# Loading w1 in full rows, a 512-column xn, and row tiles that trade banks, in a one-core attention and MLP kernel

## Chip, core, metric

The kernel runs on one NeuronCore of one Trainium2 chip, in one launch. The metric is the device time of one execution in microseconds (us). Before the change it is 152.92 us, the median of 3 runs (152.84 to 153.02). Each run also carries a state: "slow" when it is over 1.5% above the fastest run of the same kernel. Ratios use fast runs alone; a median that is quoted is of all runs of a kernel, and says so where one of them was slow. The profiled executions are single runs, and profile times count from the first instruction, so a profile's span is about 1.7 us shorter than the time of the same run.

## The reference

```
x:[1,2048,448] bf16,  H=16 heads of 28,  F=1792
xn    = layernorm(x)
q,k,v = xn @ wqkv
phi_q = concat(softmax(q @ w_phi), softmax(-q @ w_phi))      # per head, 56 features; phi_k likewise
kv, z = sum_s phi_k * v,  sum_s phi_k
att   = ((phi_q @ kv) / (phi_q @ z + 1e-6)) @ wo
mlp   = silu(xn @ w1) @ w2
out   = x + att + mlp
```

## The kernel before

S = 2048 is cut into 16 row tiles of 128 rows ("tiles" 0 to 15) and 4 chunks of four tiles. D = 448 is seven blocks of 64. Every matmul is issued as a pair: one on array rows 0 to 63 ("LO", q = 0) and one on rows 64 to 127 ("HI", q = 1), with the two results in two different banks of PSUM, the memory that matmuls write to. A list scheduler in the kernel source orders each engine's instructions when the program is built. After that the order is fixed. In the profile after, VectorE kept to its list: two copies whose input PE had written by 19.9 us started at 22.33, behind an instruction that waited for a load until 21.77.

The names used below: F1 is xn @ w1 with silu, F2 is h @ w2, V and QK are the projections, FT and FM prepare the weights of QK (transpose the qk half of wqkv, multiply by w_phi), X brings xn into transposed form (xT), U and WO are the attention output at the end.

xT must hold each 64-block on both halves of the partitions. So xn is written with every block twice, 896 columns, and from tile 4 on one transposing DMA on the sync engine (SP) turns a whole tile:

```python
def LN_b(t, parts=((0, NS),), od=False):                      # NS = 7 blocks
    ...
        dst = xnd[:, t % NX, a * 128:b * 128].rearrange("p (s r n) -> p s r n", s=b - a, r=2)
        src = xs.rearrange("p (s n) -> p s n", s=NS)[:, a:b, None, :].broadcast_to([128, b - a, 2, 64])
        ... e.tensor_scalar(dst, src, mean, rstd, subtract, mult)      # VectorE

def X_dma(t):                                                 # tiles 4..15
    dstx = xT[:, c % NXC, :, j * 128:(j + 1) * 128]
    src = xnd[:, t % NX, :]
    P.dma(lambda e: e.dma_start_transpose(out=dstx, in_=src), ..., issue=1230.0, fixed=3200.0)
```

w1 lies as halves: LO partitions hold columns 0 to 895 and HI partitions 896 to 1791, so each load covers 64 partitions. The bulk loads (x of tiles 4 to 7 among them) follow at marks in the stream of matmuls:

```python
w1v = B_w1.rearrange("(s p) f -> p s f", p=64)
def load_w1(a, b, after=None):
    load(w1_sb[LO, a:b, :], w1v[:, a:b, 0:896], ...)
    load(w1_sb[HI, a:b, :], w1v[:, a:b, 896:1792], ..., eng="act")
...
# F1, a pair: one 64-block s, two output tiles
pair([(bank(2 * sl + q)[:, 0:n], w1_sb[HALF[q], s, i * 128:(i + 1) * 128],
       xT[HALF[q], c % NXC, s, ...], s == 0, s == NS - 1) for q in range(2)], n, "f1")
...
load(wv_sb[LO], ..., after=marks[2])
load(wv_sb[HI], ..., after=marks[3])
load_x(4, 6, after=marks[4])
load(w2_sb[:, 0:7], ..., after=marks[5])
load_x(6, 8, after=marks[7])
load(w2_sb[:, 7:14], ..., after=marks[8])
...
for t in range(4, 8):
    LN(t); X_dma(t)                 # layernorm and transpose for chunk 1
```

The order of the tensor engine's stages at the start is: F1 of chunk 0 with FT and FM inside, V, QK and F2 of chunk 0, then F1 of chunk 1.

The softmax here doesn't subtract the row's maximum and nothing guards it: scores larger than these inputs give would overflow.

## Time and profile before

| | before |
|---|---|
| time, median | 152.92 us |
| span of the profile | 151.6 us |
| PE busy | 142.8 us |
| first F1 matmul | 6.67 us |
| first V, first QK matmul | 24.29, 27.04 us |
| first F1 matmul of chunk 1 | 37.63 us |
| from the first QK matmul to the end ("the tail") | 124.5 us |

The page's table of busy time and its chain of work that ended last (shares of the span), of the kernel before:

```profile
PE 142.8 (94%) x2118; PEld 88.3 (58%) x2118; DVE 96.7 (64%) x179; ACT 84.4 (56%) x106; POOL 83.9 (55%) x95
...
PE 91%; DMA 4%; issue 1%; ACT 1%; DVE 0%; DVEq 0%; ACTq 0%
```

The same chain in order of time, before; columns are start, us, what:

```profile
20.71 1.57 issue
22.28 125.66 PE psum L432 x1774
```

From 22.28 to 147.94 us the tensor engine (PE) works without a break. What is lost lies before that. The PE timeline, before; columns are start, busy us, engine, line, operation, output<-input, shapes, count, and in brackets the idle time before the group and what ended it:

```profile
6.67 0.62 PE L432 MATMUL psum<-xT,w_sb 64*128 64x128 bf16 x16 [0.74 <-DMA w_sb<-in_B_w_dram]
...
8.73 1.04 PE L432 MATMUL psum<-xT,w_sb 64*128 64x128 bf16 x16 [1.32 <-DMA w_sb<-in_B_w_dram]
...
22.28 0.23 PE L432 MATMUL psum<-BD,phT 64*128 64x56 bf16 x4 [1.57 <-issue]
...
24.29 1.49 PE L432 MATMUL psum<-wv_sb,xT 64*128 64x448 bf16 x14
...
27.04 2.82 PE L432 MATMUL psum<-wqk,xT 64*128 64x448 bf16 x28
...
37.63 6.22 PE L432 MATMUL psum<-xT,w_sb 64*128 64x512 bf16 x56
```

Two waits for w1 and one stall stand before 22.28 us. Between the two w1 waits and after them the granted clock (the share of the tensor engine's full clock that the profile reports as granted) falls too: 0.5 from 8.04 to 11.45 us. The windows table, before; columns are stretch, its length, then busy us (and instructions) of PE, PEld, DVE, ACT, POOL, then the granted PE clock, the DMA share and GB/s:

```profile
8.70:12.04 3.34, 3.31 (x62) 3.06 (x63) 1.94 (x8) 0.33 (x1) 0.55 (x1) 0.59 1.06 287
```

```profile
L570 SPq DMA_TRANSPOSE xT<-xnd x4: 1286/1296/1327, 29.2 to 33.3; - x4
DMA to landing us min/median/max: 3.0/3.1/3.2
```

Each of these transposing DMAs holds the SP queue for 1.30 us. Four of them for chunk 1 take 5.34 us in a row. The last one, issued at 33.26, landed at 36.22 us by the trace. F1 of chunk 1 starts at 37.63. So there is a deadline here, and it is met with 1.4 us to spare.

### The profile page before, as it was taken

How to read it: one execution, taken by the hardware profiler on the slowest of the kernel's cores; microseconds unless marked ns; L12 is line 12 of the kernel's file. 1: busy time of each engine (PE TensorE's matmuls, PEld its weight loads, DVE VectorE, ACT ScalarE, POOL GpSimd, SP SyncE). 2: the span in 40 equal slices, each digit the busy share in tenths (PEclk: the TensorE clock that was granted, in tenths of full speed). 3: DMA queues.
4: the chain of work that ended last, by engine and by line, in shares of the span. 5: the costliest groups of instructions: out<-in, count | busy, mean ns of one | idle time of the engine just before them, and what ended most of it. 6: DMA issues, size and time to landing. Idle time of an engine off the chain costs nothing.

```text
span 151.6 us, 4915 instructions
## 1 busy us (share of the span) xinstructions
PE 142.8 (94%) x2118; PEld 88.3 (58%) x2118; DVE 96.7 (64%) x179; ACT 84.4 (56%) x106; POOL 83.9 (55%) x95
## 2 busy tenths in 40 slices
PE   6769959999999999999999999999999999999990
PEld 2379957555556555555555556565556666666550
DVE  2747548699998376990129697874047694848633
ACT  3115748988955976895779587678573102011110
POOL 3307000706999996969902899999991402222130
PEclk9959999999999999999999999999999999999999
DMA  3996895093772997239781023333376344863323
GB/s 79 255 272 178 227 316 206 4 169 73 225 93 42 137 173 153 69 97 157 158 183 35 0 63 80 69 74 69 73 107 79 81 123 124 49 191 73 102 84 121
DMA packets 43678, 18.42 MB, mean 122 GB/s; under 512 B 36680, under 2 KB 43400, under 8 KB 43656
## 3 DMA queue, kind: packets, MB, share of 16 engines
q1 hardware_dynamic: 43000, 17.19, 53.6%
q10 hardware_dynamic: 656, 0.92, 2.4%
q8 instruction: 17, 0.28, 0.8%
q14 instruction: 5, 0.04, 0.1%
HBM read 7.48 MB, written 1.84 MB: 61 GB/s over the span
## 4 chain that ended last, share of the span: by engine, by line
PE 91%; DMA 4%; issue 1%; ACT 1%; DVE 0%; DVEq 0%; ACTq 0%
PE psum L432 90%; DMA w_sb<-in_B_w_dram 4%; PE psum L445 1%; ACT L496 1%; DVE x_sb L752 0%; DVEq L1020 0%; ACTq L463 0%
## 5 line engine op out<-in xcount | busy, mean ns | idle before, releaser
L640 POOL TENSOR_TENSOR E<-E,Rk 128x896 bf16<-128x896 bf16 x32 | 53.3, 1699 | 8.7 <-ACT E L450 6.3
L432 PE MATMUL psum<-xT,w_sb 64*128 64x512 bf16 (+2 forms) x522 | 48.1, 331 | 2.1 <-DMA w_sb<-in_B_w_dram 2.1
L432 PE MATMUL psum<-w_sb,hT 64*128 64x448 bf16 x448 | 45.2, 349 | 0.0
L450 ACT ACTIVATE hT<-psum 128x1024 bf16<-128x1024 f32 (+1 forms) x32 | 28.9, 917 | 12.8 <-PE psum L432 12.0
L432 PEld LDWEIGHTS psum<-xT,w_sb 64*128 64x128 bf16 x522 | 26.5, 98 | 15.4 <-DMA w_sb<-in_B_w_dram 1.7
L432 PEld LDWEIGHTS psum<-w_sb,hT 64*128 64x128 bf16 x448 | 24.1, 94 | 16.6
L633 DVE TENSOR_REDUCE Sk<-E 128x64 f32<-128x1792 bf16 x16 | 31.9, 2004 | 2.4 <-ACT E L450 2.3
L450 ACT ACTIVATE E<-psum 128x896 bf16<-128x896 f32 x32 | 27.4, 916 | 6.2 <-PE psum L432 6.0
L450 ACT ACTIVATE xT<-psum 128x448 f32<-128x448 f32 (+2 forms) x12 | 5.7, 481 | 33.8 <-PE psum L432 21.9
L432 PE MATMUL psum<-wqk,xT 64*128 64x448 bf16 x224 | 23.6, 349 | 0.0
L704 POOL TENSOR_TENSOR xT<-xT,x_sb 128x448 f32<-128x448 f32 x8 | 8.3, 1034 | 24.9 <-ACT xT L450 24.9
L432 PEld LDWEIGHTS psum<-wqk,xT 64*128 64x128 bf16 x224 | 12.2, 94 | 8.6
L557 DVE TENSOR_SCALAR xnd<-x_sb,mv,rstd 128x896 bf16<-128x896 bf16 (+2 forms) x18 | 11.1, 656 | 9.1 <-POOL rstd L547 9.1
L547 POOL TENSOR_TENSOR rstd<-ve,neghalf 128x1 f32<-128x1 f32 x16 | 8.8, 564 | 8.7 <-DVE ve L545 8.4
L692 POOL TENSOR_TENSOR Ye<-Ye,x_sb 128x448 f32<-128x448 f32 x8 | 8.2, 1035 | 7.7 <-DVE Ye L690 7.7
L432 PE MATMUL psum<-wv_sb,xT 64*128 64x448 bf16 x112 | 11.9, 349 | 0.0
L539 DVE BATCH_NORM_STATS2 st<-x_sb 128x6 f32<-128x448 bf16 x16 | 9.5, 608 | 3.4 <-DMA x_sb<-in_A_x_dram 3.4
L432 PE MATMUL psum<-wo_sb,E 64*128 64x448 bf16 x112 | 11.3, 349 | 0.0
L690 DVE TENSOR_TENSOR Ye<-psum,Ye 128x448 f32<-128x448 f32 x8 | 5.0, 621 | 9.0 <-ACT Ye L450 8.9
L729 DVE TENSOR_TENSOR E<-psum,rden 128x224 bf16<-128x224 f32 x32 | 10.3, 383 | 0.3
L545 POOL TENSOR_SCALAR ve<-mv 128x1 f32<-128x1 f32 x12 | 2.3, 216 | 12.4 <-DVE mv L543 12.4
L432 PEld LDWEIGHTS psum<-wo_sb,E 64*128 64x128 bf16 x112 | 6.2, 94 | 4.4
(42 smaller groups left out, 102.0 us busy)
## 6 DMA issues: line engine op xcount, KB each, us to landing
out_dram<-x_sb SPq DMA_DIRECT2D x8, 224.0 KB, 2.2
w_sb<-in_B_w_dram SPq DMA_DIRECT2D x2, 784.0 KB, 6.7
x_sb<-in_A_x_dram SPq DMA_DIRECT2D x2, 448.0 KB, 4.5
wv_sb<-in_A_wqkv_dram SPq DMA_DIRECT2D x2, 392.0 KB, 4.7
wo_sb<-in_A_wo_dram SPq DMA_DIRECT2D x14, 56.0 KB, 2.2
w_sb<-in_B_w_dram SPq DMA_DIRECT2D x3, 224.0 KB, 5.4
w_sb<-in_B_w_dram ACTq DMA_DIRECT2D x3, 224.0 KB, 6.1
phT<-in_A_wqkv_dram SPq DMA_DIRECT2D x1, 448.0 KB, 5.6
```

Source lines behind the costliest of these rows:

```text
L432: ins = e.matmul(dst, lhsT, rhs, start=st, stop=sp, skip_group_check=True)
L450: return P.op("act", d_act(n), lambda e: e.activation(dst, src, func, scale=scale), reads=reads or [src], writes=writes or [dst], table=ta ...
L539: P.op("dve", 630, lambda e: e.bn_stats(st6[:, t, :], xs), [xs], [st6[:, t, :]], name="bnst", ordered=od)
L545: lambda e: e.tensor_scalar(ve[:, t:t + 1], mv[:, t, 1:2], EPS_LN, None, ALU.add),
L547: P.op("pool", 580, lambda e: e.tensor_tensor(rstd[:, t:t + 1], ve[:, t:t + 1], neghalf[:], ALU.pow), [ve[:, t:t + 1], neghalf[:]], [rstd[ ...
L557: lambda e, dst=dst, src=src: e.tensor_scalar(dst, src, mv[:, t, 0:1], rstd[:, t:t + 1], ALU.subtract, ALU.mult),
L633: dve(lambda e: e.tensor_reduce(Sk[:, t % 3, :].rearrange("p (h g) -> p h g", g=2), Er, AXL.X, ALU.add), d_dve(1792), [Er], [Sk[:, t % 3, ...
L640: pool(lambda e, Eh=Eh, Rb=Rb: e.tensor_tensor(Eh, Eh, Rb, ALU.mult), 1770, [Eh, Rh], [Eh], "phi%d" % qk)
L690: dve(lambda e: e.tensor_tensor(y, b, y, ALU.add), d_dve(D), [b, y], [y], "ye_d")
L692: pool(lambda e: e.tensor_tensor(y, y, x_sb[:, t, :], ALU.add), 1110, [y, x_sb[:, t, :]], [y], "ye_x")
L704: pool(lambda e: e.tensor_tensor(y, y, x_sb[:, t, :], ALU.add), 1110, [y, x_sb[:, t, :]], [y], "yl_x")
L729: dve(lambda e, dst=dst, src=src, rb=rb: e.tensor_tensor(dst, src, rb, ALU.mult), d_dve(224), [src, r], [dst], "o")
```

## The change

The intent: load w1 faster by using all 128 partitions with full rows of 3584 bytes, so that the first matmuls don't wait. A block of 128 rows then holds the needed 64-block of one half and the wrong one for the other half. In chunk 0 F1 therefore runs in two phases: in phase 0 LO and HI each write one bank, in phase 1 they trade the two banks (`h = q ^ ph`), with a wait of PE on itself where a bank changes hands. The missing halves of w1 are loaded late (`w1r`), for chunks 1 to 3. xn shrinks to 448 columns plus the first 64 again (512), because LO and HI now share 128-column windows that overlap by 64. A tile from chunk 1 on then needs windows at even and at odd blocks, hence two transposing DMAs. The bulk loads get a new order and a limit of three in flight. Smaller parts: a preload of the silu table, and a schedule search with 60 randomly shaken passes. The core of the diff, with cuts:

```diff
-        xnd = sb("xnd", [128, NX, NS * 128], BF16)
+        xnd = sb("xnd", [128, NX, 512], BF16)
...
+        chain = []
+        def chained(*args, **kw):
+            chain.append(load(*args, after=chain[-3], **kw))
+        def load_w1(b, eng):
+            chain.append(load(w1_sb[:, 2 * b:2 * b + 2, :].rearrange("p h f -> p (h f)"), B_w1[b * 128:(b + 1) * 128, :],
+                              128 * FF * 2, 2 * FF, f"w1{b}", eng=eng, issue=480))
...
+        def load_bulk():
+            for b in range(NB):
+                ... chained(wraw[0:r, b, 8:904], A_wqkv[...], ..., f"wqk{b}")
+            ... # the four small w_phi loads
+            for q in range(2):
+                chained(wv_sb[HALF[q]], wvv, D * D * 2, D * 2, f"wv{q}")
+            chained(x_sb[:, 4:6, :], ..., "x4")
+            ... # w2, two loads
+            chained(x_sb[:, 6:8, :], ..., "x6")
+            ... # w2, two loads
...
-        def LN_b(t, parts=((0, NS),), od=False):
+        def LN_b(t, parts=((0, D), (D, 512)), od=False):
...
+        def xw(q, c, s, c0, c1):
+            return xT[HALF[q], c % NXC, (s - q) % NS, c0:c1]
...
-            dstx = xT[:, c % NXC, :, j * 128:(j + 1) * 128]
-            src = xnd[:, t % NX, :]
-            P.dma(lambda e: e.dma_start_transpose(out=dstx, in_=src), ..., issue=1230.0, fixed=3200.0)
+            for w0, src, dur in ((0, xnd[:, t % NX, :], 720.0), (1, xnd[:, t % NX, 64:448], 560.0)):
+                dstx = xT[:, c % NXC, w0:NS:2, j * 128:(j + 1) * 128]
+                P.dma(lambda e, dstx=dstx, src=src: e.dma_start_transpose(out=dstx, in_=src), ...,
+                      issue=dur, fixed=dur + 2000.0)
...
+        def F1ph(ph, sl, col, i, x0, n, first, bs=(0, 1, 2), six=True):
+            for b in bs:
+                for q in range(2):
+                    h = q ^ ph
+                    mms.append((bank(2 * sl + h)[:, col:col + n], w1_sb[HALF[q], 2 * b + h, i * 128:(i + 1) * 128],
+                                xw(q, 0, 2 * b + q, x0, x0 + n), ...))
+                op = pair(mms, n, "f1")
+                swapped(op, (2 * sl, 2 * sl + 1), ph)        # PE waits for itself where a bank changes side
...
+        for q in range(2):
+            load(w1_sb[HALF[q], 1 - q:6:2, :], ..., f"w1r{q}")    # the missing halves, after chunk 0's last F1
```

## The prediction

> **What bounds the kernel now.** The tensor engine. The page's busy table gives PE 142.8 of 151.6 us; the chain of waits is PE from 22.28 us to 147.94 us without a break. What can be won lies before that. The windows table shows: 5.35 to 8.70 us, PE busy 1.29 of 3.35; 8.70 to 12.04 us, busy but at a granted clock of 0.59; 20.70 to 22.28 us, idle. The PE timeline names the gaps: 0.74 us (6.64) and 1.32 us (8.7) until a w1 load lands, and 1.57 us "issue", in the middle of a group of small matmuls with no semaphore between. I count the work from the first F1 matmul to the first V matmul at the trace's spacing (56 ns a pair at 128 columns, 108 at 256, about 28 for transposes): some 13 us; it takes 17.6 us (6.64 to 24.28).
>
> **What the change does.**
> 1. w1 rate and order. In the trace's packet records, w1's 1792-byte packets (64 partitions per load) take about 127 ns; the same size into 128 partitions takes 78 ns, and 3584-byte packets in the later x load 140 ns. So w1's 1.6 MB should flow at nearly 400 instead of some 270 KB/us. With five loads instead of eight, issued sooner on two queues, I estimate both first row blocks landed near 5.8 us and all of w1 by 7.7 us (before: about 11.9). Both w1 waits vanish, and with them most of the half-clock window, worth about 1.3 us.
> 2. xn of 512 instead of 896 columns (719 ns now; I estimate 0.45 us), and 5 windows instead of 7 transposed first for tiles 0 and 1: F1 starts near 6.0 us instead of 6.64. The two left-out windows come back later as 4 pairs, 0.1 us.
> 3. Cost: banks change row tile. [...] hence waits of PE on itself. No run shows their price yet. Most have 200 ns or more of other matmuls between; estimate 0.4 us in all.
> 4. The late halves of w1 (0.69 MB more) go after chunk 0's last F1, some 10 us before chunk 1 needs them: free. The bulk loads, three in flight, should all have landed by about 20 us (before: 26.5), ahead of their use. Two transposing DMAs per tile in place of one: same bytes, off the path.
> 5. The 1.57 us stall looks like instruction fetch behind bulk DMA. [...] the trace agrees with 17 packets of 16,384 bytes on one instruction queue, the one before the stall starting at about 19.9 us. In the new stream the same block is needed earlier, still under dense DMA: it may shrink, stay or grow.
>
> **Sum.** 0.65 (start) + 2.1 (w1 waits, part of the first term's cause, so 1.4 net) + 1.3 (clock) + up to 1.6 (fetch; I count 0.6) - 0.4 (swaps) - 0.6 (waits for evictions and slots around tile 3) = about 2.9 us. Nearly all on the critical path, since everything behind is back-to-back PE work and shifts along. I predict 150.0 us, 148.5 to 151.8 in 8 of 10 cases; faster by over 2%: 0.46; within 2%: 0.49; slower: 0.05.
>
> **What would show it.** F1 from about 6.0 us; no PE wait on w1; granted clock 1.00 between 8.7 and 12; the first QK matmul near 24.0 us instead of 27.0; the rest unbroken.
>
> **What would make it wrong.** Costlier bank swaps (20 at 0.2 us would eat it); a longer fetch stall; chunk 1's F1 waiting for its transposed x or its late w1; the granted clock still falling. If fetch stalls disappear and swaps are free, 148.5.

## More of the kernel before

F1 of chunk 1 needs xT of tiles 4 to 7, all four.

The SP timeline and the view of the tile xT, both in the stretch around chunk 1's transposes, before (the second gives durations in ns as min/median/max, then the first and last start):

```profile
29.22 5.34 SPq L570 DMA_TRANSPOSE xT<-xnd  x4
```

## The result, and the profile after

The changed kernel takes 159.07 us (median of 4 runs, 158.52 to 162.9, the last of them slow), the kernel before 152.88 (4 runs, 152.59 to 153.02). The ratio is 1.0395, with a 95% interval of 1.0355 to 1.0436: slower. A ratio is the mean time of one kernel's fast runs over that of the other kernel's fast runs of the same rounds, so it is not quite the ratio of the medians quoted.

| us, from the profiles | before | after |
|---|---|---|
| span | 151.6 | 157.6 |
| first F1 matmul | 6.67 | 6.37 |
| chunk 0's F1 done | 24.25 | 20.85 |
| x of tiles 4 and 5, of 6 and 7 landed | 20.49, 24.55 | 21.77, 25.71 |
| first QK matmul | 27.04 | 27.97 |
| last transpose for chunk 1 landed | 36.22 | 41.95 |
| tail from the first QK matmul | 124.5 | 129.7 |

The loss adds up as 0.93 us before QK and 5.14 us after it, 6.07 together, which is the difference of the spans. Of the 5.14, 4.82 are two waits, shown below.

The page of the changed kernel, busy time and chain:

```profile
PE 144.3 (92%) x2118; PEld 87.2 (55%) x2118; DVE 105.6 (67%) x194; ACT 85.4 (54%) x109; POOL 84.4 (54%) x95
...
PE 67%; DMA 11%; SPq 7%; ACT 5%; DVE 4%; issue 2%; POOL 1%; DVEq 0%; ACTq 0%
```

PE works about as long as before. But the chain, which was PE for 91%, is PE for only 67% now, and SP's queue and DMA have come into it. In order of time, after:

```profile
16.31 5.45 DMA x_sb<-in_A_x_dram
21.79 0.63 DVE st L566
22.42 0.67 DVE phT L838 x2
...
23.13 5.09 PE psum L447 x68
...
35.64 1.26 SPq L599
36.94 1.26 SPq L599
38.24 2.43 DMA xT<-xnd
40.67 1.47 issue
42.14 15.43 PE psum L447 x202
...
65.92 2.65 DMA xT<-xnd
68.58 0.09 issue
68.67 85.36 PE psum L447 x1258
```

The PE timeline, after:

```profile
6.37 0.52 PE L447 MATMUL psum<-xT,w_sb 64*128 64x128 bf16 x8 [0.26 <-ACT xT L465]
...
7.37 3.98 PE L447 MATMUL psum<-xT,w_sb 64*128 64x128 bf16 x88
...
16.74 0.38 PE L447 MATMUL psum<-BD,phT 64*128 64x56 bf16 x16 [0.93 <-DMA BD<-in_A_w_phi_dram]
...
23.13 0.38 PE L447 MATMUL psum<-BD,phT 64*128 64x56 bf16 x16 [2.28 <-DVE phT L838]
23.35 2.44 PE L447 MATMUL psum<-wv_sb,xT 64*128 64x448 bf16 x14
...
27.97 2.81 PE L447 MATMUL psum<-wqk,xT 64*128 64x448 bf16 x28
...
38.56 0.38 PE L447 MATMUL psum<-xT,w_sb 64*128 64x512 bf16 x2
42.14 3.20 PE L447 MATMUL psum<-xT,w_sb 64*128 64x512 bf16 x28 [3.20 <-issue]
...
68.67 1.69 PE L447 MATMUL psum<-xT,w_sb 64*128 64x512 bf16 x14 [1.62 <-DMA xT<-xnd]
```

The waits for w1 are gone, and the half clock at 8.7 us with them. Chunk 0's F1 is done 3.4 us earlier (some 0.2 of that because one group of FM products comes after it now). Then four things happen.

1. At 20.85 us PE waits 2.28 us for VectorE. The VectorE (DVE) timeline, after, shows for what:

```profile
18.34 0.49 DVE L646 COPY xT<-psum 128x256 bf16<-128x256 bf16 x2 [0.43 <-PE psum L460]
21.79 0.63 DVE L566 BATCH_NORM_STATS2 st<-x_sb 128x6 f32<-128x448 bf16 x1 [2.96 <-DMA x_sb<-in_A_x_dram]
22.33 0.74 DVE L838 COPY phT<-psum 128x512 bf16<-128x512 bf16 x2
```

The eviction that PE needs (L838) stands in VectorE's order behind the statistics of tile 4 (L566), and these wait for x of tiles 4 and 5 until 21.77 us. VectorE has nothing else to do for 2.96 us.

2. After that idle time the granted clock is 0.50 from 23.7 to 27.1 us, and the V pairs take 2.44 and 2.06 us instead of 1.49 each: 1.5 us more. The windows table, after:

```profile
8.70:12.04 3.34, 3.34 (x76) 2.85 (x72) 2.97 (x11) 2.29 (x3) 2.21 (x6) 1.00 0.70 200
...
23.70:27.10 3.40, 3.40 (x36) 1.66 (x34) 1.65 (x5) 1.90 (x4) 1.44 (x4) 0.50 0.74 233
```

So QK starts 0.9 us later than before, although F1 was 3.4 us ahead.

3. The SP timeline and the view of the tile xT, after:

```profile
29.70 11.10 SPq L599 DMA_TRANSPOSE xT<-xnd  x8
```

```profile
L599 SPq DMA_TRANSPOSE xT<-xnd x8: 1256/1264/1934, 29.7 to 39.5; - x8
DMA to landing us min/median/max: 2.4/2.5/4.3
```

A transposing DMA of 3 or 4 windows holds the queue for 1.26 us, one of 7 windows held it for 1.30. Half the work costs nearly the same. Eight of them take 11.1 us instead of 5.34, the last lands at 41.95, and F1 of chunk 1, which began its first pair at 38.56, goes on at 42.14. The timeline calls those 3.20 us "issue", but they end 0.19 us after that landing.

The eight begin only 0.5 us later than the four did (29.70 against 29.22), so at chunk 1 it is the doubled time on the queue, and hardly the late x, that moves the last landing by 5.7 us.

4. In chunk 2 PE waits 1.62 us for a transposing DMA, and is labelled so. But here a second cause is needed, the order of SP's list:

```profile
54.95 1.23 SPq L478 DMA_DIRECT2D wo_sb<-in_A_wo_dram  x2
56.22 11.27 SPq L599 DMA_TRANSPOSE xT<-xnd  x8
```

The eight stand behind two loads of wo, and SP is idle from 49.24 us until the first of these, which waits for PE, goes out. In the kernel before chunk 2's transposes begin at 47.29 us, ahead of wo. In e2 and e4 below, eight of them begin at 47.72 and 46.26 us, and chunk 2 has no wait. No run moved this order alone.

### The profile page after: what moved, and what is told of

It is laid out like the page before. It is cut to its first block, busy times and chain, and to the rows that moved or that the text cites. A ratio compares the mean times of both kernels' runs of the same rounds, so it can differ in the third digit from the quotient of the medians.

```text
span 157.6 us, 4961 instructions
## 1 busy us (share of the span) xinstructions
PE 144.3 (92%) x2118; PEld 87.2 (55%) x2118; DVE 105.6 (67%) x194; ACT 85.4 (54%) x109; POOL 84.4 (54%) x95
## 4 chain that ended last, share of the span: by engine, by line
PE 67%; DMA 11%; SPq 7%; ACT 5%; DVE 4%; issue 2%; POOL 1%; DVEq 0%; ACTq 0%
PE psum L447 67%; DMA x_sb<-in_A_x_dram 8%; SPq L599 5%; DMA xT<-xnd 3%; SPq L478 2%; ACT E L465 2%; DVE Sk L693 1%; DVE st L566 1%; POOL E L557 1%; ACT L465 1%; DVE Ye L750 1%; ACT Ye L465 1%; ACT vb L465 1%; DVE phT L838 0%; POOL rstd L574 0%
## 5 line engine op out<-in xcount | busy, mean ns | idle before, releaser
L447 PE MATMUL psum<-xT,w_sb 64*128 64x512 bf16 (+2 forms) x522 | 47.2, 324 | 5.1 <-issue 3.2
L465 ACT ACTIVATE hT<-psum 128x1024 bf16<-128x1024 f32 (+1 forms) x29 | 28.4, 993 | 15.0 <-PE psum L447 14.9
L447 PEld LDWEIGHTS psum<-xT,w_sb 64*128 64x128 bf16 x522 | 25.0, 94 | 19.2 <-issue 5.7
L465 ACT ACTIVATE E<-psum 128x896 bf16<-128x896 f32 x32 | 27.4, 916 | 5.6 <-PE psum L447 5.2
L465 ACT ACTIVATE xT<-psum 128x448 f32<-128x448 f32 (+3 forms) x14 | 6.6, 475 | 32.1 <-PE psum L447 27.8
L447 PE MATMUL psum<-wqk,xT 64*128 64x448 bf16 x224 | 23.7, 349 | 0.0
L583 DVE TENSOR_SCALAR xnd<-x_sb,mv,rstd 128x64 bf16<-128x64 bf16 (+3 forms) x34 | 20.8, 667 | 0.5 <-POOL rstd L574 0.5
L566 DVE BATCH_NORM_STATS2 st<-x_sb 128x6 f32<-128x448 bf16 x16 | 9.6, 613 | 8.1 <-DMA x_sb<-in_A_x_dram 8.1
L447 PE MATMUL psum<-wv_sb,xT 64*128 64x448 bf16 x112 | 13.5, 382 | 0.0
L447 PEld LDWEIGHTS psum<-wv_sb,xT 64*128 64x128 bf16 x112 | 6.3, 101 | 4.7 <-issue 1.3
```

Of the source, the lines that this page charges most:

```text
L447: ins = e.matmul(dst, lhsT, rhs, start=st, stop=sp, skip_group_check=True)
L465: return P.op("act", d_act(n), lambda e: e.activation(dst, src, func, scale=scale), reads=reads or [src], writes=writes or [dst], table=ta ...
L566: P.op("dve", 630, lambda e: e.bn_stats(st6[:, t, :], xs), [xs], [st6[:, t, :]], name="bnst", ordered=od)
L583: lambda e, dst=dst, src=src: e.tensor_scalar(dst, src, mv[:, t, 0:1], rstd[:, t:t + 1], ALU.subtract, ALU.mult),
```

## Theories

The texts below call the leading theory T: the doubled issue time of transposing DMAs, fed by x of tiles 4 to 7 that comes late, misses the deadline of chunk 1's F1; the late x also causes the head's gap through VectorE's order. Head gap and tail wait are then two faces of one deadline.

The main rival, R1, is that VectorE is the late one. The changed kernel's xn instructions (448 and 64 columns) take 10.5 + 10.5 us in sum where 14 instructions of 896 columns took 9.5, and single ones of 448 columns stretch from 0.4 to 1.88 us beside GpSimd's multiplies. What makes them stretch is not shown. If R1 were right, the transposes would come late because xn does, whatever their number. Where an expectation sets another rival against T, it says there what that rival claims.

All eleven kernels below gave correct results.

## Experiments

### e1_a_onetr: one transposing DMA per tile, in the changed kernel

```diff
-xnd = sb("xnd", [128, NX, 512], BF16)
+xnd = sb("xnd", [128, NX, NS * 128], BF16)
 def LN_b(...):
+    if t >= 4: ... the 896-column form of the kernel before; return
-    return xT[HALF[q], c % NXC, (s - q) % NS, c0:c1]
+    return xT[HALF[q], c % NXC, s if c else (s - q) % NS, c0:c1]
 def X_dma(t):
-    two transposing DMAs
+    the single one of the kernel before
```

> The changed kernel, but row tiles 4 to 15 get their transposed x as in the kernel before: 896 columns of xn, one transposing DMA per tile. Theory T (a transposing DMA holds the SP queue for 1.26 us whatever its size, so two per tile double the chain before F1 of chunks 1 and 2): the waits of 3.2 us and 1.6 us at the first F1 of chunks 1 and 2 vanish, the head stays as it is (V starts near 23.4 us); about 154.2 us against 159.1 for the change, 0.8 to 1% above the kernel before. Rival R2 (the transposes are late because x4 to x7 and LN are late): the waits stay above 2 us in sum and the time stays above 157.

Measured: 152.49 us (151.67 to 154.24, one of four slow), the kernel before in the same rounds 152.79; ratio 0.9948 [0.9893, 1.0004]. The PE timeline of this run has no wait at chunks 1 and 2:

```profile
22.11 0.38 PE L447 MATMUL psum<-BD,phT 64*128 64x56 bf16 x16 [1.23 <-DVE phT L846]
...
35.87 6.21 PE L447 MATMUL psum<-xT,w_sb 64*128 64x512 bf16 x56
```

The tail is 124.5 us again. The run gave back more than the 5.1 us of the tail, because its head was better as well: x of tiles 4 and 5 came at 20.74 us instead of 21.77, the gap was 1.23 instead of 2.28 us, and no half clock followed. The head's gain has a different cause from the tail's, since the edit changes no load and no instruction of chunk 0 (see e5). The edit puts both the single transpose and the 896-column xn back, so it does not yet separate T from R1. It also puts chunk 2's transposes ahead of the wo loads again (they begin at 46.06 us).

### e2_b_split: two transposing DMAs per tile, in the kernel before

```diff
-    dstx = xT[:, c % NXC, :, ...]; src = xnd[:, t % NX, :]; one transposing DMA
+    for a, b in ((0, 4), (4, NS)):
+        dstx = xT[:, c % NXC, a:b, ...]; src = xnd[:, t % NX, a * 128:b * 128]; a transposing DMA
```

> The kernel before, with nothing changed but each transposing DMA cut in two (4 and 3 column windows). Theory T: each half still takes some 1.26 us to issue, so chunk 1's last one lands about 5.2 us later against a slack of 1.4 us: F1 of chunk 1 waits 3.5 to 4 us, chunk 2 perhaps 0 to 2 us; 156.5 to 158.5 us. Rivals (xn form, bulk order, bank swaps): no part of them is in this kernel, so within 1% of 152.9.

Measured: 157.45 us (155.96 to 157.92), ratio 1.0264 [1.0196, 1.0332], formally "unclear" only against the 2% line. xn is untouched here (726 ns for 896 columns). The xT view and the PE timeline of this run:

```profile
L571 SPq DMA_TRANSPOSE xT<-xnd x8: 1254/1257/1504, 28.7 to 38.0; - x8
```

```profile
37.09 1.04 PE L432 MATMUL psum<-xT,w_sb 64*128 64x512 bf16 x8
41.13 4.42 PE L432 MATMUL psum<-xT,w_sb 64*128 64x512 bf16 x24 [3.01 <-DMA xT<-xnd]
```

Same bytes, same windows, twice the instructions: 4.7 us lost and a tail of 129.4 us, almost the changed kernel's 129.7. That is the doubling alone, with nothing of w1, of the swaps or of xn. The wait of 3.01 us and the one half-clock window after it (42.1 to 45.5 us, some 1.7 us) account for most of it. That the two tails are nearly equal is a coincidence: the changed kernel has no half clock after its wait, but a second wait of 1.62 us at chunk 2, which is missing here.

### e3_b_xn2: xn in two instructions, in the kernel before

```diff
+    if t >= 4:
+        for r in range(2):          # the two copies of each block, 7 x 64 columns each
+            e.tensor_scalar(dst[:, :, r, :], src, ...)
```

> The kernel before, but xn of tiles 4 to 15 in two instructions of 448 columns without the repeated read, as the change's xn is. Rival R1 ([...] in the changed kernel they took up to 1.88 us beside the phi multiplies, 0.37 to 0.40 us without): several xn take 1.2 us or more beside the phi multiplies, transposes of chunk 2 come later, and if R1 matters the time rises by 1 us or more (over 154). Theory T: the durations may stretch, but the time stays within 0.5 us of 152.9.

Measured: 152.89 us (152.3 to 153.36), ratio 0.999 [0.9951, 1.003]. This was meant to put R1's cost into the kernel before, and failed to: an instruction that writes 64-column pieces took 491 ns in the mean and 506 at most, though 11 of the 24 ran beside the phi multiplies. So it tests nothing about R1 but one point, that the stretching depends on the form of the output (491 ns here, 766 ns in the mean for the changed kernel's contiguous 448 columns):

```profile
L559 DVE TENSOR_SCALAR xnd<-x_sb,mv,rstd 128x448 bf16<-128x448 bf16 x24 | 10.2, 491 | 8.8 <-issue 6.6 <-POOL rstd L547 2.2
```

### e5_a_concat: e1 with xn as two plain 448-column copies

One transposing DMA as in e1, but xn in the changed kernel's form: contiguous columns, two instructions.

```diff
-    dst = the 896-column form, every block twice
+    for a in (0, D): e.tensor_scalar(xnd[:, t % NX, a:a + D], xs, ...)
+    # windows of the transposed tile renumbered to match: w = s - q mod 7; w // 2 or (w + 7) // 2
```

> As e1 (the changed kernel, one transposing DMA per tile for tiles 4 to 15), but xn of these tiles written twice as plain 448 columns side by side, the form of instruction that in the changed kernel stretched to 1.88 us beside the phi multiplies (e3 did not show it: its 7 x 64 pattern stayed at 0.50 us). Rival R1 (this stretching is part of the loss): xn instructions of 1.2 us or more return in chunks 2 and 3, and the time is 1 us or more over e1's 152.5. Theory T plus H: they return, but the time stays within 0.7 us of e1, as the deadline in chunk 1 comes before the phi multiplies.

Measured: 154.26 us (153.45 to 154.37), the kernel before 152.55; ratio 1.0095 [1.005, 1.0141]. The groups of VectorE, this run:

```profile
L584 DVE TENSOR_SCALAR xnd<-x_sb,mv,rstd 128x448 bf16<-128x448 bf16 x24 | 16.6, 756 | 3.3 <-POOL rstd L574 3.3
```

The mean of 756 ns is close to the changed kernel's 766, and six instructions took over 1 us, the longest 1.87 (in the changed kernel four of 448 columns and five of 64, the longest 1.88). So R1's cost is in this kernel. Its tail is 124.5 us all the same, with no wait at chunks 1 and 2. By the time that the expectation had set as the test, the run speaks for R1, as it is 1.8 us slower than e1. The trace decides otherwise. It puts all of that into the head, where the edit doesn't reach: gaps of 0.92 and 2.31 us, a half clock from 24.0 to 27.4, x of tiles 4 and 5 landed at 21.85 us. That is the changed kernel's own head. R1 is rejected: VectorE's stretched instructions are off the critical path. The trace of the changed kernel says the same. The 448-column xn of chunk 1 take 0.37 to 0.40 us there, unstretched, and the last xn of chunk 2 is written at 54.87 us, before its first transpose is issued at 56.22.

What e1 and e5 together show besides: the same loads landed 1.1 us apart in two runs on two chips, with the same order of instructions on PE, VectorE and ScalarE up to QK, and the head moved by 2.8 us, a half clock included (QK at 25.28 or at 28.05). The head hangs on the landing of one load.

### e4_a_x4first: x of tiles 4 to 7 loaded earlier, in the changed kernel

The four w_phi loads come first too, so it is two repairs in one: of the 2.28 us gap and of the 0.93 us wait for w_phi. Both transposing DMAs stay.

```diff
 def load_bulk():
+    the four w_phi loads
     wqk, four loads
-    the four w_phi loads
-    wv, two loads
     chained(x_sb[:, 4:6, :], ...)
-    w2, two loads
     chained(x_sb[:, 6:8, :], ...)
+    wv, two loads
+    w2, two loads
     w2, two loads
```

> The changed kernel with another order of the bulk loads alone: w_phi first, then x4 and x6 straight after the qk weights, before wv. Theory H (the 2.3 us gap before V and the half clock after it come from VectorE standing in order behind LN of tile 4, whose x landed at 21.8 us; the 0.9 us gap from w_phi): both gaps vanish, clock 1.0 there, V starts near 20 us instead of 23.4, and the whole comes 3 to 4 us earlier, 155 to 156 us, still with the waits at the first F1 of chunks 1 and 2. If the gaps come from something else (instruction fetch, bank swaps), V still starts after 22.5 us and the time stays within 1 us of 159.

Measured: 152.57 us (152.13 to 153.25), ratio 0.9975 [0.9935, 1.0015]. x landed at 15.04 and 17.54 us. V and QK start at 22.04 and 25.0 us, the transposes begin at 24.23 instead of 29.70, and the wait at chunk 1 is down to:

```profile
36.81 6.24 PE L447 MATMUL psum<-xT,w_sb 64*128 64x512 bf16 x56 [1.05 <-ACT Ye L465]
```

The label names ScalarE, but the last transpose landed at 36.61, 0.2 us before. This returned more than expected: nearly all of the loss, with the doubled transposes in place. V had been expected near 20 us and came at 22.04, because the head kept one gap, 1.89 us at 17.08, of the old kind: PE waits for a cast (L857) that stands in VectorE's order behind statistics waiting for x of tiles 6 and 7.

### e6_a_both: e1 and e4 together

> e1 and e4 together: one transposing DMA per tile, and w_phi, x4, x6 loaded early. e1 and e4 each gave back 6.5 us of the 6.2 us lost. If both act on one chain with one deadline (x4 lands, LN, transposes, first F1 of chunk 1), the second repair adds little: 150.5 to 152 us, and no wait on the transposes is left (e4 still waited 1.0 us). If they were two separate losses, 146 us.

Measured: 151.02 us (150.78 to 152.3), the kernel before 152.55; ratio 0.9912 [0.9862, 0.9962]. Each edit alone had returned about 6.5 us of the changed kernel's time, and both together return only 1.5 us more than one (by the ratios to the kernel before, only 0.5 to 1). They don't add, because either end of the chain x lands → layernorm → transposes → F1 of chunk 1 makes the same deadline. QK starts at 23.94 us, where the prediction had it ("near 24.0"). The tail is 125.5 us, 0.9 longer than in e1; the windows of the trace put that into the last 30 us.

### e7_a_unchained: the changed kernel without the limit of three loads

```diff
-    chain.append(load(*args, after=chain[-3], **kw))
+    chain.append(load(*args, **kw))
```

> The changed kernel with the limit of three bulk loads in flight taken away, their order kept. If the limit makes x4 land late (22.1 us), x4 lands at or before 20 us, and the time falls by 2 us or more below 159. If it is the place in the order, behind both wv loads, x4 still lands after 21 us and the time stays above 157.5. With more loads queued, instruction fetch may stall the tensor engine again by 1 to 2 us near 17 to 21 us.

Measured: two of four runs were slow, the two fast ones took 156.62 and 156.87 us, and no ratio was computed. x of tiles 4 and 5 came at 18.22 instead of 21.77 us, QK began at 26.31, and the tail was still 128.6 us, with 2.24 us of waiting for transposes at chunk 2. In exchange the last part of w1 came at 10.0 us instead of 8.77. Of the stall of 1 to 2 us that had been thought possible, 0.74 us labelled "issue" came, up to 21.72 us. The first branch of the expectation held: the limit is a part of the delay of x, 3.6 us. The order of the loads is the larger one: e4 brought x 6.7 us earlier with the limit in place.

### e9_a_gate: only the order on VectorE mended, in the changed kernel

The statistics of tiles 4 to 7 may start only after the evictions that PE waits for.

```diff
 def LN_st(t, od=False):
-    P.op("dve", ...bn_stats...)
+    o = P.op("dve", ...bn_stats...)
+    if 4 <= t < 8: o.deps.add(gate[0].id)      # gate: the last FT eviction on VectorE
```

> The changed kernel with one thing moved: LN of tiles 4 to 7 may not stand on VectorE before the last two evictions of the transposed qk weights. Loads and transposes as in the change. If the head's gap and the wait at chunk 1 are one chain with one deadline (x4 lands at 22 us, LN, eight transposes of 1.26 us, first F1 of chunk 1), the 2.3 us gap before V and the half clock vanish, the first QK comes near 24.5 us instead of 28.0, and the wait at chunk 1 grows by as much, to 6 us or more: 157.5 to 160 us, no gain. If they are separate losses, the wait stays near 3.2 us and the time falls to about 155.5.

Measured: 159.43 us (158.82 to 160.2), the kernel before 152.89; ratio 1.0415 [1.0356, 1.0475], so no better than the changed kernel. The 2.28 us gap is gone and QK starts at 25.1 us, 2.9 earlier. Nothing of that reaches the end:

```profile
37.08 0.39 PE L447 MATMUL psum<-xT,w_sb 64*128 64x512 bf16 x2 [0.29 <-issue]
40.77 7.59 PE L447 MATMUL psum<-xT,w_sb 64*128 64x512 bf16 x54 [3.30 <-DMA xT<-xnd]
```

The last transpose landed at 40.57 us. The wait was 3.3 us where 6 or more had been expected; PE arrived 1.5 us earlier than after the change (37.08 against 38.56), while the transposes ended 1.4 us earlier. The rest of the head's gain went into smaller gaps on the way (0.29 us and 0.76 us) and into a half clock from 40.6 to 44.0, after the wait. So the forecast of the time held and that of the wait did not. By the deadline alone this run should have gained 1.4 us (PE goes on at 40.77 instead of 42.14), and the half clock took it back. What it shows is the smaller statement: of 2.9 us won in the head, nothing was left at the end.

### e8_a_best: e6, with x of tiles 4 to 7 in one load still earlier, and the order on VectorE mended

```diff
 e6, and
     for b in range(NB):
+        if b == 2: chained(x_sb[:, 4:8, :], ...)      # one load, ahead of the last two wqk loads
         chained(wraw[...], ...)
+    statistics of tiles 4 to 7 only after the evictions of X_rest
```

> e6 with two mends of the order: x4 to x7 in one load of full 3584-byte rows ahead of the last two qk weight loads, and LN of tiles 4 to 7 held on VectorE until the late windows of tiles 0 and 1 are evicted, so that nothing that TensorE needs stands behind an x load. Expected: no wait of TensorE over 0.5 us between 7 us and the end, V from about 20.2 to 20.8 us, 149.8 to 150.8 us, 1.3 to 2% below the kernel before. If gaps of 1 us or more stay in the head, the in-order VectorE was not their whole cause.

Measured: 150.3 us (149.9 to 153.0, one of six slow), the kernel before 152.55 in the same rounds; ratio 0.9855 [0.9811, 0.9899]. It is the best version found, and it beats both kernels, by 1.45% the kernel before. Its profiled execution (151.42 us) was the slowest of the five fast runs, and shows the one loss left in it:

```profile
7.57 0.87 PE L447 MATMUL psum<-xT,w_sb 64*128 64x128 bf16 x14 [1.00 <-DMA w_sb<-in_B_w_dram]
```

The second w1 block landed late, at 7.52 us, and a half clock followed from 7.7 to 11.1 us. V came at 22.22 and QK at 25.18 us instead of V by 20.8 at the latest, the tail was 124.5 us. No other wait of over 0.2 us is left after 7 us.

### e10_a_best3: e8 with the second w1 load on SP's queue

```diff
-load_w1(1, "act")
+load_w1(1, "sp")
```

> e8 with the second w1 load issued on the SP queue behind the first, instead of beside it on the ACT queue, so that the row blocks land in the order in which F1 uses them. In e8's profile the second block landed at 7.8 us, TensorE waited 1.0 us and its clock was halved for a window of 3.4 us. Expected: the second block lands before 6.8 us, no wait on w1, granted clock 1.0 in the head, first QK near 23.3 us instead of 25.2, 149.3 to 150.2 us. If the landing is scattered by something else, no difference from e8 (150.3).

Measured: 151.46 us (149.85 to 152.14, one of six slow), ratio 0.9881 [0.983, 0.9931]. The block landed at 7.62 us, and PE waited 0.94, 0.55 and 0.77 us for loads. The expectation failed. In the profiles of the eight kernels with the changed loads on the original queues, the block landed between 6.0 and 6.6 us six times, and at 7.52 and 7.95 us twice. Why is open.

### e11_b_w2late: the w2 loads later, in the kernel before

This is for the 1.57 us stall at 20.71 us that the profile calls "issue". The prediction took it for instruction fetch held up by bulk loads.

```diff
 load_x(4, 6, after=marks[4])
-load(w2_sb[:, 0:7], ..., after=marks[5])
 load_x(6, 8, after=marks[7])
-load(w2_sb[:, 7:14], ..., after=marks[8])
+load(w2_sb[:, 0:7], ..., after=marks[9])
+load(w2_sb[:, 7:14], ..., after=marks[10])
```

> The kernel before with the two w2 loads issued later (after the fifth and sixth F1 of chunk 0's second half), the order on all other engines unchanged. If its 1.57 us stall at 20.7 us is instruction fetch queued behind these 0.8 MB loads, the 16,384-byte packet before it starts earlier than 19.9 us and the stall shrinks below 0.6 us; the time falls by about 1 us to 151.5 to 152.3, unless w2 then comes late for F2. If the stall stays over 1 us, the fetch waits for something else.

Measured: 152.85 us (152.47 to 153.39), the kernel before 152.89; ratio 0.9993 [0.9949, 1.0038]. In the profile the stall shrank to 0.41 us, with the same order of instructions on PE, and the packet of instructions ahead of it started at 18.75 instead of 19.88 us:

```profile
21.45 0.23 PE L432 MATMUL psum<-BD,phT 64*128 64x56 bf16 x4 [0.41 <-issue]
```

The profiles of e2 and e3, with the loads and the order on PE of the kernel before, have the stall too: 1.02 us after a packet at 19.19, and 1.24 us after one at 19.44. So in four profiles the stall grows with the start of that packet. This agrees with the fetch explanation, but the timed runs show no gain. What the stall costs stays open.

## Why the prediction was wrong

It had 150.0 us; it was 159.07. By its points:

1. w1. Right in the main. The prediction had w1's first blocks at about 5.8 us and all of it at 7.7; they landed at 5.95 and 6.27, the last at 8.77. (Its 127 ns for a packet is the mean of those that began between 5 and 7 us; from 2.2 to 9.9 us the median is 114, and from 3 to 5 us, still to 64 partitions, 74. So how far the partitions set the packet's time stays open.) Both waits and the early half-clock window went away, and chunk 0's F1 ended 3.4 us sooner.
2. xn and the start. F1 began at 6.37, not 6.0 us. The cost of xn was wrong: "I estimate 0.45 us", but 448 plus 64 columns took some 0.39 + 0.29 us undisturbed and, with the stretching beside GpSimd, 766 + 665 ns in the mean. For tile 0, which F1 waits for, it was 0.96 us in three pieces, against 0.87 in two before. The stretching cost no time, as e5's tail shows.
3. Bank swaps. The size was too high. Twenty pairs of 128 columns and 24 of 256 took 3.82 us, swaps included (7.37 to 11.19 us). At the spacing of the kernel before, 56 and 108 ns, they would take 3.71. So the swaps with PE's waits on itself cost about 0.1 us there, where the prediction had 0.4 in all, the author's estimate. That a swap needs such a wait is not shown, as no run leaves it out. No run swaps banks back to back, without other matmuls between.
4. This is the step that failed: "The bulk loads, three in flight, should all have landed by about 20 us (before: 26.5), ahead of their use. Two transposing DMAs per tile in place of one: same bytes, off the path." Both sentences were wrong.
   - x of tiles 4 and 5 stands behind wqk and both wv loads and landed at 21.77 us, later than the 20.49 before; w2 landed at 29.26. VectorE's order turned this into 2.28 us of idle PE and 1.5 us of half clock. e4 and e9 show it: with x (and w_phi) earlier in the list, QK comes 3.0 us sooner, and with VectorE's order alone mended, 2.9.
   - The price of these DMAs on the queue goes by their number and not by their bytes: 1.26 us for each of 3 or 4 windows, 1.30 for one of 7, and 1.25 (median of 16) for those that turn the 1024 columns of phi. No run has a larger one. Eight of them take 11.1 us instead of 5.34. e2 puts this part alone into the kernel before and loses 4.7 us; e1 and e5 take it out of the changed kernel, with two forms of xn, and the waits are gone. At chunk 2 the wait needed the late place in SP's list as well.
5. Fetch. The traces before and after each have 17 packets of 16,384 bytes on the instruction queue, of 0.9 to 1.7 us. The profile after shows no such stall on PE at that place. The 0.6 us that the prediction counted can't be checked, since e11's timed runs showed no value in it.

The sum hid a second fault: "everything behind is back-to-back PE work and shifts along". An unbroken chain of PE work says that nothing was late *at that pace*. The transposes had 1.4 us to spare. To bring PE forward by the predicted 2.9 us would have run into them even with one transpose per tile, unless their input came sooner as well. The prediction named "chunk 1's F1 waiting for its transposed x" among what could go wrong, but gave it no number, although both numbers (33.26 plus 3 us of landing, and 37.63) were in the profile before.

How the 6.07 us of the profiles divide: F1 of chunk 0 ends 3.40 us earlier, in spite of a new wait of 0.93 us for w_phi, which is needed 3.6 us sooner than before (FM's first product at 16.74 instead of 20.32 us). From there to QK it takes 7.12 us instead of 2.79. Of these 4.33 us more, 2.28 are the gap, some 1.7 the half clock (on V and on one FM group) and 0.2 the FM group that moved; the rest is the overlap of F1's end with the next matmuls. That is the 0.93 us at QK. Then come 3.20 + 1.62 us of waiting for transposes, and 0.32 in pieces.

Idle time can cost twice: after some gaps the granted clock is 0.5 for a while. The windows at half clock are 3.4 us long (8.0 to 11.5 us before the change, 23.7 to 27.1 after it, 42.1 to 45.5 in e2, 40.6 to 44.0 in e9, 7.7 to 11.1 in e8), and the idle gaps before or in them were 2.3 to 3.3 us, just 1.0 in e8, and in the kernel before 0.74 and 1.32. Other gaps of the same size cost none: 1.23 us in e1, and even the 3.20 us at chunk 1 of the changed kernel. What decides between the two is not shown. So a gap's price here is its length, and sometimes 1.5 us more (on the two V groups of the changed kernel).

What stays open: why the second w1 block lands 1 to 2 us later in some profiles; the extra 0.9 us at the end of e6; the worth of the stall of e11; and what the order on SP's queue alone is worth at chunk 2. The wait at chunk 1, its cause and the return of the time are shown by e1, e2, e4, e5 and e6. That the doubling is needed for the wait at chunk 2 is shown by e5, which has single transposes behind the same two wo loads (from 52.92 us) and no wait; that it is not enough, by e2 and e4.

## What to carry to other kernels

Before you call something off the critical path, write down its slack: when its last piece lands and when its consumer comes. Here 1.4 us of slack was to take 5.8 us more of issue, and at the same time the consumer was to come 2.9 us sooner. Count transposing DMAs by the time that they hold the issuing queue (here 1.26 us for 3 or 4 windows, 1.30 for 7), not by their bytes, and load first what starts the longest chain of dependent steps (here x of the next tiles, ahead of weights that are needed later). Look in an engine's list for an instruction that waits for a late load: here one on VectorE delayed the copies behind it, long ready, and PE stood idle for 2.28 us.
